# Experts that run by their count: a test around a loop that no expert enters, code moved between instruction pages, and fp32 conversions spread over the experts

## The chip, the cores and the metric

One core of a Trainium2 chip. The time is the device time of one launch in microseconds (us); of several runs the median counts. Five engines work side by side, each with its own list of instructions: PE (TensorE, matmuls; PEld is its weight load), DVE (VectorE), ACT (ScalarE), POOL (GpSimd) and SP (SyncE). They wait for each other through semaphores only. Loads and stores go through DMA queues that SP, ACT and POOL feed. The code of an engine comes through a DMA queue of its own too (q8 and q14 in the profile).

## The reference

Three layers in a row over 2304 tokens of 512 numbers; arithmetic in fp32.

```python
# 1. attention: B, H, S, D = 4, 8, 576, 64; each query sees the 64 keys up to itself
scores = where((rel >= 0) & (rel < 64), q @ k.T / sqrt(D), -1e9)
x = softmax(scores) @ v                    # to [2304, 512]
# 2. experts: 8 of them, FF 1024
do = x @ w_skip > 0                        # other tokens pass unchanged
e_idx = argmax(x @ w_gate); p = softmax(x @ w_gate)
x[do] += p[e_idx] * (relu(x[do] @ w1[e_idx]) @ w2[e_idx])
# 3. a last feed-forward layer, 512 to 2048 to 512, for all tokens
h = x @ w_in
out = where(h >= 1, h, where(h <= -1, 0, (h + 1)**2 / 4)) @ w_out
```

How many tokens an expert has is known only at run time. With these inputs expert 2 has more than 128 and at most 256, expert 4 more than 256 and at most 384, the other six at most 128.

## The kernel before

Attention and the routing of the tokens come first (to 117.6 us), then the experts (to 276.1), a transition (to 287), and the last layer, which takes the rest. At the very start PE runs WARM matmuls of WARM_COLUMNS columns on ones while the first loads come in.

**Experts.** The tokens of an expert are cut into tiles of 128. `tile_of(e, t)` runs a tile t of expert e through `ffn`: the matmuls `ha` and `hb` with w1 (L753), ACT's relu that evacuates them (`h`, L760), their transposes (`hTp`, L766), the matmuls `y` with w2 (L792), and `mx`, which adds the weighted result to the tokens (DVE, L797). `load_x` gathers a tile's tokens by index, `store_x` scatters them back, both on POOL's DMA queue. Tile 0 of each expert always runs. Tile 1 stands in an If on the expert's count (L860), tile 2 in a second (L864), and further tiles in a For_i whose bounds are `3 * P` and the count (L868). In the built program these are branches on each engine: the instructions are all there, and an engine whose expert has no such tile jumps over them, on PE some 390 instructions for L860.

**fp32 by parts.** Every fp32 operand of a matmul is split into a high and a low part that add up to it: ACT writes the high part (L132 and L137), DVE, in some cases POOL, the low one (L133 and L138). `hT` and `mxT` are such splits of a tile's data, `w` those of weights. The splits of weights are ahead of their use by a ring of 14 pairs, and are laid out by the hooks of `ffn`: functions that are called at fixed places of a tile 0 ("start", "a", "b", 0, 1, 2) and put instructions there. `mine` are the pairs of this expert's second half, `nxt` those of the next expert, `splits` the first seven left over.

**Conversions.** The weights of the last layer (w_in, w_out, named `raw` when loaded) come as 64-bit numbers, and eight pieces of them are converted to fp32 during the experts: `convert` is five DVE operations on 128x512 each (L168; before, the first two run through a generator, `convert_by_parts`, L191 and L168). SLOW says how many of the pieces in EARLY are converted by expert e: those from SLOW[e] to SLOW[e+1]. They run in hook "a" and, if left, in hook 2; the two first ones in expert 0 by hook "start" and "b".

**Order of loads.** `to_load` is a list of the pieces in order of need, and `load_raws` starts the next when a buffer is free: on SP's queue, twice on ACT's in the beginning.

**Code.** An engine's instructions stand in the order of the Python code; the loop bodies of later tiles are part of it, at each expert. All of it lies in DRAM and comes to the engine in pieces.

Of the kernel before, what the change touches and what calls it, by code (L numbers as in the profile page):

```python
# [4 lines left out]

# [6 lines left out]
F32 = mybir.dt.float32  # L12
F32R = mybir.dt.float32r
BF16 = mybir.dt.bfloat16
I32 = mybir.dt.int32
I64 = mybir.dt.int64
AF = mybir.ActivationFunctionType
# [31 lines left out]

EARLY = tuple((U_IN + j, c) for j in range(2) for c in range(4))  # L50
EARLIEST = 2
BEFORE = 6

LATE = tuple(
    (u, c) for u in (U_OUT, U_OUT + 1, U_IN + 2, U_OUT + 2, U_IN + 3, U_OUT + 3) for c in range(4)
)
AHEAD_OF_IT = 3

SLOW = (2, 4, 5, 6, 6, 7, 8, 8, 8)
ROUTES = (3, 3, 3, 3, 3, 3)  # L60
WARM = 97
WARM_COLUMNS = 80
WGW = 32
AHEAD = 3
KEEP = (4, 8, 70, 2, 36)
# [5 lines left out]
def moe_chain(  # L71
# [54 lines left out]
    def take_raw(key):  # L126
        r, n = raws.pop(key)
        left[n] = max(left.values(), default=0) + 1
        return r
# [12 lines left out]
    def convert_ops(w, r, mag=None):  # L142

        low, high = r[:, :, 0], r[:, :, 1]
        wf = w.bitcast(F32)
        v = nc.vector
        ops = [
            partial(  # L150
                v.tensor_scalar, w, high, 3, 0x3FFFFFFF, op0=ALU.logical_shift_left, op1=ALU.bitwise_and
            ),
            partial(
                v.scalar_tensor_tensor, w, high, -0x40000000, w, op0=ALU.bitwise_and, op1=ALU.bitwise_or
            ),
            partial(
                v.scalar_tensor_tensor, w, low, 29, w, op0=ALU.logical_shift_right, op1=ALU.bitwise_or
            ),
        ]
        if mag is None:  # L160
            ops.append(partial(v.tensor_single_scalar, high, high, 0x7FFFFFFF, ALU.bitwise_and))
            mag = high.bitcast(F32)
        ops.append(partial(v.scalar_tensor_tensor, wf, mag, LEAST, wf, op0=ALU.is_ge, op1=ALU.mult))
        return ops
# [13 lines left out]
    def do_convert(u, c, into):  # L178
# [1 line left out]
            early[u, c] = into.tile([P, 2, 512], F32, tag="early", name=f"c{u}_{c}")  # L180
        convert(early[u, c // 2 * 2][:, c % 2].bitcast(I32), take_raw((u, c)))
        load_raws()

    def convert_by_parts(todo, into):

        for _, u, c in todo:
            if c % 2 == 0:
                early[u, c] = into.tile([P, 2, 512], F32, tag="early", name=f"c{u}_{c}")
            for op in convert_ops(early[u, c // 2 * 2][:, c % 2].bitcast(I32), raws[u, c][0]):
                yield  # L190
                op()  # L191
            take_raw((u, c))
            if at_once[0]:
                load_raws()

    def work(todo, engines):

        for eng in engines[: len(todo)]:
            what, u, c = todo.pop(0)
            if what == "s":  # L200
                do_split(u, c, eng)
            else:
                do_convert(u, c, early_pool[0])
# [495 lines left out]
    with ExitStack() as ectx:  # L699
# [3 lines left out]
        def bank(i, shape, name):  # L703
            return psp.tile(shape, F32, tag=f"bank{i}", name=name)
# [7 lines left out]
        def load_x(at, name, tag, bufs):  # L712
            x = mp.tile([P, RW], F32, tag=tag, name=f"mx{name}", bufs=bufs)
            nc.gpsimd.memset(tick, 0.0)
            dma = nc.gpsimd.indirect_dma_start(
                out=x, out_offset=None, in_=x1,
                in_offset=bass.IndirectOffsetOnAxis(ap=at, axis=0),
            )
            apart(dma, "gathers", ("scatters",))
            return x  # L720
# [17 lines left out]
            split(xT[:, 0], xT[:, 1], px)  # L738
            return xT

        def ffn(e, x, xT, name, hooks=(), b0=0):

            hooks = dict(hooks)

            def at(k):
                if k in hooks:
                    hooks[k]()

            def mm1(ph, j, lo, hi):
                seq = [(c, a, b) for p in (PASSES[:2], PASSES[2:]) for c in range(KD) for a, b in p]  # L750
                for n in range(lo, hi):
                    c, a, b = seq[n]
                    nc.tensor.matmul(  # L753
                        ph, lhsT=xT[:, a, c, :], rhs=halves[4 * e + j, c][:, b, :],
                        start=(n == 0), stop=(n == len(seq) - 1),
                    )

            def evac(ph, j):
                h = mp.tile([P, 512], F32, tag="h", name=f"h{name}_{j}")
                nc.scalar.activation(h, ph, AF.Relu)  # L760
                return h

            def tr(h, j):
                pt = bank(b0 + j, [P, 4, P], f"hTp{name}_{j}")
                for c in range(4):
                    nc.tensor.transpose(pt[:, c, :], h[:, c * P : (c + 1) * P], ident)  # L766
                hT = mp.tile([P, 2, 4, P], F32R, tag=f"hT{j}", name=f"hT{name}_{j}", bufs=1)
                split(hT[:, 0], hT[:, 1], pt)
                return hT

            at("start")
            pa = bank(b0, [P, 512], f"ha{name}")
            mm1(pa, 0, 0, 12)
            ha = evac(pa, 0)
            pb = bank(b0 + 1, [P, 512], f"hb{name}")
            mm1(pb, 1, 0, 6)
            hTa = tr(ha, 0)
            at("a")
            mm1(pb, 1, 6, 12)
            hb = evac(pb, 1)  # L780
            py = bank(b0 + 2, [P, 512], f"y{name}")
            hT = [hTa, None]

            seq = [(c, a, b) for p in (PASSES[:2], PASSES[2:]) for c in range(4) for a, b in p]
            for j in range(2):
                for n, (c, a, b) in enumerate(seq):
                    if j == 0 and n == 6:
                        hT[1] = tr(hb, 1)
                        at("b")
                    if j == 1 and n % 3 == 0:  # L790
                        at(n // 3)
                    nc.tensor.matmul(  # L792
                        py, lhsT=hT[j][:, a, c, :], rhs=halves[4 * e + 2 + j, c][:, b, :],
                        start=(j == 0 and n == 0), stop=(j == 1 and n == len(seq) - 1),
                    )
            y = x[:, 0:DM]
            nc.vector.scalar_tensor_tensor(y, py, x[:, DM:RW], y, op0=ALU.mult, op1=ALU.add)  # L797
# [14 lines left out]

        rawp.append(ectx.enter_context(tc.tile_pool(name="raw2", bufs=RAWS[2])))
        early_pool.append(ectx.enter_context(tc.tile_pool(name="earlier", bufs=len(EARLY) // 2)))
        parts = convert_by_parts(converts, early_pool[0])
        fetch(0, 0)
        work(splits, [dve] * 3)
        pre(0, 0)
# [8 lines left out]
        for e in range(NE):  # L827

            mine = pairs(8 * e + RING - 8, 8 * e + 8)
            nxt = pairs(8 * e + 8, 8 * e + RING)  # L830
            if e == 0:
                mine, nxt = [], []
            elif e + 1 == NE:
                nxt = [("s", u, c) for u, c in EARLY if c % 2 == 0]
            turn = [("c", u, c) for u, c in EARLY[SLOW[e] : SLOW[e + 1]]]
            last = e + 1 == NE
            def second():

                xeT[e, 1] = mp.tile([P, 2, KD, P], F32R, tag="mxT", name=f"mxT{e}_1")
                with tc.If(counts[e] > P):  # L840
                    prep(xe[e, 1], f"{e}_1", "mxTl", xeT[e, 1])

            hooks = {
                "start": lambda: (
                    work(splits, [dve] * len(splits)),
                    list(islice(parts, BEFORE)) if e == 0 else None,
                    work(mine, [dve, dve]),
                ),
                "a": lambda: (
                    work(turn, [dve]),  # L850
                    work(nxt, [dve, dve] if last else [dve]),
                ),
                "b": lambda: (list(parts) if e == 0 else None, work(nxt, [dve, dve])),
                0: lambda: None if last else (pre(e + 1, 0), fetch(e + 1, 1)),
                1: lambda: (second(), work(nxt, [dve, dve])),
                2: lambda: (work(nxt, [dve]), work(turn, [dve])),
            }
            tile_of(e, 0, hooks)
            store_x(at_of(e, 0), xe[e, 0])
            with tc.If(counts[e] > P):  # L860
                fetch(e, 2)
                tile_of(e, 1)
                store_x(at_of(e, 1), xe[e, 1])
                with tc.If(counts[e] > 2 * P):  # L864
                    pre(e, 2)
                    tile_of(e, 2)
                    store_x(at_of(e, 2), xe[e, 2])
                    with tc.For_i(3 * P, counts[e], P) as r:  # L868
                        at = mp.tile([P, 1], I32, tag="at", name=f"at{e}", bufs=1)
                        nc.vector.tensor_copy(at, idx[:, bass.ds(r // P + e * NT, 1)])  # L870
                        x = load_x(at, f"{e}_l", "mxl", 1)
                        ffn(e, x, prep(x, f"{e}_l", "mxTl"), f"{e}_l", b0=4)
                        store_x(at, x)
            if e + AHEAD < NE:
                fetch(e + AHEAD, 0)

# [280 lines left out]
```

## Time and profile before

| | |
|---|---|
| median of 3 runs | 709.76 us (709.02 to 711.63) |
| the profiled execution: its time | 707.99 us |
| the profiled execution: its span | 706.3 us |
| attention and routing | 117.6 us |
| experts | 158.5 us |
| transition | 10.9 us |
| last layer | 419.3 us |

The span is the time from the first to the last instruction in the profile; the run's own time is 1.7 us longer. Times in the views are us from the span's start. `PEclk` is the granted TensorE clock as a share of full speed. A wait "<- issue" is one in which the profile shows nothing that the engine waited for.

### The profile page before, as it was taken

How to read it: one execution, taken by the hardware profiler on the slowest of the kernel's cores; microseconds unless marked ns; L12 is line 12 of the kernel's file. 1: busy time of each engine (PE TensorE's matmuls, PEld its weight loads, DVE VectorE, ACT ScalarE, POOL GpSimd, SP SyncE). 2: the span in 40 equal slices, each digit the busy share in tenths (PEclk: the TensorE clock that was granted, in tenths of full speed). 3: DMA queues.
4: the chain of work that ended last, by engine and by line, in shares of the span. 5: the costliest groups of instructions: out<-in, count | busy, mean ns of one | idle time of the engine just before them, and what ended most of it. 6: DMA issues, size and time to landing. Idle time of an engine off the chain costs nothing.

```text
span 706.3 us, 12298 instructions
## 1 busy us (share of the span) xinstructions
PE 672.3 (95%) x4622; PEld 573.1 (81%) x4622; DVE 426.4 (60%) x806; ACT 384.5 (54%) x765; POOL 92.6 (13%) x137
## 2 busy tenths in 40 slices
PE   7999977899999799998999999999999999999997
PEld 6777766677787575897989999999999999999995
DVE  4788864997782499787888864444433443333332
ACT  5787642374761485565666655454444454445443
POOL 3256545031230211000000000000000000000000
PEclk9999998999999999999999999999999999999999
DMA  8999944898791393632423202120300030002002
GB/s 210 312 277 290 301 149 112 282 329 329 214 356 59 113 314 122 213 110 76 148 87 94 76 0 61 31 59 31 91 1 0 1 90 0 1 1 45 1 1 45
DMA packets 34502, 88.81 MB, mean 126 GB/s; under 512 B 6958, under 2 KB 8110, under 8 KB 34420
## 3 DMA queue, kind: packets, MB, share of 16 engines
q1 hardware_dynamic: 25344, 71.72, 33.7%
q10 hardware_dynamic: 6756, 9.45, 3.9%
q0 software_dynamic: 2320, 6.58, 2.7%
q8 instruction: 47, 0.77, 0.5%
q14 instruction: 35, 0.29, 0.1%
HBM read 75.65 MB, written 13.12 MB: 126 GB/s over the span
## 4 chain that ended last, share of the span: by engine, by line
PE 55%; DVE 3%; ACT 1%; issue 1%; ACTq 0%; DVEq 0%
PE h L914 27%; PE po L942 26%; PE spare L1030 1%; PE p2x L904 1%; DVE c L935 1%; DVE c L932 1%; ACT q L925 1%; DVE w L138 0%; DVE gs L933 0%; DVE q L924 0%; DVE x2T L133 0%; ACT q L921 0%; DVE q L928 0%; ACT part L951 0%; ACT w L137 0%
## 5 line engine op out<-in xcount | busy, mean ns | idle before, releaser
L914 PE MATMUL h<-x2T,w 128*128 128x384 f32 x1152 | 218.2, 338 | 1.0 <-DVE x2T L133 0.9
L942 PE MATMUL po<-w,gs 128*128 128x512 f32 x864 | 217.3, 396 | 1.6 <-ACT w L137 0.9
L914 PEld LDWEIGHTS h<-x2T,w 128*128 128x128 f32 x1152 | 204.7, 188 | 10.0 <-DVE x2T L133 1.7
L942 PEld LDWEIGHTS po<-w,gs 128*128 128x128 f32 x864 | 159.6, 188 | 32.0 <-ACT w L137 1.2
L921 ACT ACTIVATE q<-h 128x384 f32<-128x384 f32 x96 | 47.0, 489 | 107.8 <-PE h L914 106.5
L924 DVE TENSOR_SCALAR q<-q 128x384 f32<-128x384 f32 x96 | 34.4, 358 | 98.2 <-ACT q L921 98.0
L928 DVE TENSOR_TENSOR q<-hs,q 128x384 f32<-128x384 f32 x96 | 53.7, 559 | 49.8 <-ACT q L925 49.8
L930 ACT ACTIVATE gs<-q 128x384 fp32r<-128x384 f32 x96 | 50.5, 526 | 60.0 <-DVE q L928 60.0
L933 DVE TENSOR_TENSOR gs<-q,gs 128x384 fp32r<-128x384 f32 x96 | 53.6, 559 | 44.4 <-ACT gs L930 44.4
L137 ACT ACTIVATE w<-raw 128x1024 fp32r<-128x1024 f32 x64 | 65.1, 1057 | 26.2 <-issue 12.1
L792 PE MATMUL y<-w,hT 128*128 128x512 f32 x264 | 69.7, 403 | 1.8 <-DVE hT L133 0.7
L138 DVE TENSOR_TENSOR w<-raw,w 128x1024 fp32r<-128x1024 f32 x54 | 63.6, 1220 | 12.0 <-ACT w L137 10.0
L925 ACT ACTIVATE q<-q 128x384 f32<-128x384 f32 x96 | 50.5, 526 | 22.6 <-DVE q L924 19.1
L792 PEld LDWEIGHTS y<-w,hT 128*128 128x128 f32 x264 | 47.4, 189 | 14.5 <-issue 3.3
L360 ACT ACTIVATE pr<-s,nb 128x128 f32<-128x128 f32 x144 | 39.0, 383 | 17.0 <-DVE nb L356 17.0
L923 ACT ACTIVATE hs<-h 128x384 f32<-128x384 f32 x96 | 46.8, 487 | 0.0
L753 PE MATMUL ha<-w,mxT 128*128 128x512 f32 x132 | 35.4, 417 | 9.8 <-issue 4.9
L753 PEld LDWEIGHTS ha<-w,mxT 128*128 128x128 f32 x132 | 25.1, 197 | 19.3 <-issue 10.6
L753 PE MATMUL hb<-w,mxT 128*128 128x512 f32 x132 | 35.2, 402 | 0.0
L356 DVE TENSOR_REDUCE nb<-s 128x4 f32<-128x512 f32 x36 | 23.2, 686 | 14.8 <-PE s L349 12.5
L724 POOL DMA_INDIRECT x<-mx,idx x11 | 16.5, 1501 | 116.6 <-POOLq L860 65.1
L138 POOL TENSOR_TENSOR w<-raw,w 128x1024 fp32r<-128x1024 f32 x10 | 23.6, 2362 | 35.7 <-ACT w L137 24.7
(172 smaller groups left out, 690.9 us busy)
## 6 DMA issues: line engine op xcount, KB each, us to landing
raw<-in_wu SPq DMA_DIRECT2D x62, 512.0 KB, 6.2
raw<-in_wd SPq DMA_DIRECT2D x28, 512.0 KB, 4.0
x<-x ACTq DMA_DIRECT2D x21, 256.0 KB, 6.1
vt<-in_vs SPq DMA_DIRECT2D x36, 130.0 KB, 6.3
x<-x SPq DMA_DIRECT2D x18, 256.0 KB, 3.2
out<-out SPq DMA_DIRECT2D x36, 128.0 KB, 2.4
q<-in_qs SPq DMA_DIRECT2D x8, 512.0 KB, 5.7
kt<-in_ks SPq DMA_DIRECT2D x8, 512.0 KB, 6.9
```

The costliest lines, as they stand in the source:

```text
L137: nc.scalar.activation(t[:, 0], src, AF.Copy)
L138: eng.tensor_tensor(t[:, 1], src, t[:, 0].bitcast(F32), ALU.subtract)
L753: nc.tensor.matmul(ph, lhsT=xT[:, a, c, :], rhs=halves[4 * e + j, c][:, b, :], start=(n == 0), stop=(n == len(seq) - 1),)
L792: nc.tensor.matmul(py, lhsT=hT[j][:, a, c, :], rhs=halves[4 * e + 2 + j, c][:, b, :], start=(j == 0 and n == 0), stop=(j == 1 and n == len ...
L914: nc.tensor.matmul(ph, lhsT=halves[U_IN + m // 4, c][:, b, (m % 4) * P : (m % 4 + 1) * P], rhs=xT[:, a, c, :], start=(n == 0), stop=(n == ...
L921: nc.scalar.activation(q, ph, AF.Relu, bias=0.5, scale=0.5)
L923: nc.scalar.activation(h, ph, AF.Copy)
L925: nc.scalar.activation(q, q, AF.Square)
L928: nc.vector.tensor_tensor(q, h, q, ALU.max)
L930: nc.scalar.activation(gs[:, 0], q, AF.Copy)
L933: dve.tensor_tensor(gs[:, 1], q, gs[:, 0].bitcast(F32), ALU.subtract)
L942: nc.tensor.matmul(po[i], lhsT=gs[:, a, i * P : (i + 1) * P], rhs=w[:, b, :], start=(m == m0 and (a, b) == PASSES[0]), stop=(m == m1 - 1 a ...
```

## The change

Seven edits, of which most touch the experts:

1. The loop of tiles 3 and on stands in an If of its own, `counts[e] > 3 * P`, and counts from 0.
2. Its body uses whole fp32 operands (`prep_whole`, `mm1_whole`) instead of split ones, so it has fewer matmuls. No expert has such a tile.
3. WARM is 115 and WARM_COLUMNS 64, instead of 97 and 80.
4. SLOW spreads the conversions: by expert 0 to 7 they are 0, 1, 1, 1, 1, 1, 1, 1, 0 pieces by SLOW instead of 2, 1, 1, 0, 1, 1, 0, 0 (the first two pieces come on top, both in expert 0).
5. The first two conversions are whole ones in hook "b" and hook 1, no generator of parts any more.
6. In expert 0 the leftover weight splits stand in hook "a" instead of "start".
7. The order of loads follows SLOW.

```diff
-BEFORE = 6
...
-SLOW = (2, 4, 5, 6, 6, 7, 8, 8, 8)
+SLOW = (2, 2, 3, 4, 5, 6, 7, 8, 8)
 ROUTES = (3, 3, 3, 3, 3, 3)
-WARM = 97
-WARM_COLUMNS = 80
+WARM = 115
+WARM_COLUMNS = 64
...
+        def prep_whole(x, name):
+            px = bank(7, [P, KD, P], f"mpx{name}")
+            for c in range(KD):
+                nc.tensor.transpose(px[:, c, :], x[:, c * P : (c + 1) * P], ident)
+            xT = mp.tile([P, 2, KD, P], F32, tag="mxTl", name=f"mxT{name}", bufs=1)
+            nc.scalar.activation(xT[:, 0], px, AF.Copy)
+            return xT
...
+            def mm1_whole(ph, j):
+                w = xT[:, 1].rearrange("p c n -> p (c n)")
+                for c in range(KD):
+                    half = halves[4 * e + j, c].bitcast(F32)
+                    nc.vector.tensor_tensor(w, half[:, 0, :], half[:, 1, :], ALU.add)
+                    nc.tensor.matmul(ph, lhsT=xT[:, 0, c, :], rhs=w, start=(c == 0), stop=(c == KD - 1))
...
-        parts = convert_by_parts(converts, early_pool[0])
...
             hooks = {
-                "start": lambda: (
+                "start": lambda: work(mine, [dve, dve]),
+                "a": lambda: (
                     work(splits, [dve] * len(splits)),
-                    list(islice(parts, BEFORE)) if e == 0 else None,
-                    work(mine, [dve, dve]),
-                ),
-                "a": lambda: (
                     work(turn, [dve]),
                     work(nxt, [dve, dve] if last else [dve]),
                 ),
-                "b": lambda: (list(parts) if e == 0 else None, work(nxt, [dve, dve])),
+                "b": lambda: (work(converts, [dve]), work(nxt, [dve, dve])),
                 0: lambda: None if last else (pre(e + 1, 0), fetch(e + 1, 1)),
-                1: lambda: (second(), work(nxt, [dve, dve])),
+                1: lambda: (second(), work(converts, [dve]), work(nxt, [dve, dve])),
                 2: lambda: (work(nxt, [dve]), work(turn, [dve])),
             }
...
-                    with tc.For_i(3 * P, counts[e], P) as r:
...
+                    with tc.If(counts[e] > 3 * P):
+                        with tc.For_i(0, (counts[e] - (2 * P + 1)) // P, 1) as i:
...
+                            ffn(e, x, prep_whole(x, f"{e}_l"), f"{e}_l", b0=4, whole=True)
```

The order on DVE in expert 0 before: from the program's list of DVE's instructions, from the start of the tile to its last conversion but one. `raw` is a loaded piece, `c` the converted one, `hT_0_0` and `hT_0_1` the two halves of expert 0's tile 0, `mxT` the next tiles' data.

```order
L138 TENSOR_TENSOR w_2_2468<-raw_2_1864,w_2_2468 128x1024
L191 TENSOR_SCALAR c_0_2473<-raw_0_1983 128x512
L191 SCALAR_TENSOR_TENSOR c_0_2473<-raw_0_1983,c_0_2473 128x512 x2
L133 TENSOR_TENSOR hT_0_0_2508<-hTp_0_0_2503,hT_0_0_2508 128x512
L168 TENSOR_SCALAR c_2_2511<-raw_2_2372 128x512
L133 TENSOR_TENSOR hT_0_1_2539<-hTp_0_1_2534,hT_0_1_2539 128x512
L191 TENSOR_SCALAR c_0_2473<-raw_1_2370 128x512
L133 TENSOR_TENSOR mxT_0_2560<-mpx_0_2555,mxT_0_2560 128x512
L168 TENSOR_SCALAR c_2_2511<-raw_3_2374 128x512
L797 SCALAR_TENSOR_TENSOR mx_0_2350<-y_0_2527,mx_0_2350 128x512
```

Each `TENSOR_SCALAR c` row begins one conversion; rows of its other operations are left out. The same stretch in the changed program (its L131 is L133 here, L136 is L138, L166 is L168, L803 is L797):

```order
L131 TENSOR_TENSOR hT_0_0_2513<-hTp_0_0_2508,hT_0_0_2513 128x512
L136 TENSOR_TENSOR w_2_2516<-raw_2_1882,w_2_2516 128x1024
L131 TENSOR_TENSOR hT_0_1_2541<-hTp_0_1_2536,hT_0_1_2541 128x512
L166 TENSOR_SCALAR c_0_2544<-raw_0_2001 128x512
L131 TENSOR_TENSOR mxT_0_2563<-mpx_0_2558,mxT_0_2563 128x512
L166 TENSOR_SCALAR c_0_2544<-raw_1_2388 128x512
L803 SCALAR_TENSOR_TENSOR mx_0_2368<-y_0_2529,mx_0_2368 128x512
```

Of four conversions two are left in expert 0, both behind `hT_0_1`; the weight split moved behind `hT_0_0`.

DVE in expert 6 in the changed program, the first half of tile 0: before, the list is the same without the four rows of L166.

```order
L131 TENSOR_TENSOR hT_0_0_5040<-hTp_0_0_5035,hT_0_0_5040 128x512
L166 TENSOR_SCALAR c_2_4621<-raw_3_4632 128x512
L166 SCALAR_TENSOR_TENSOR c_2_4621<-raw_3_4632,c_2_4621 128x512 x2
L166 TENSOR_SCALAR raw_3_4632<-raw_3_4632 128x512
L166 SCALAR_TENSOR_TENSOR c_2_4621<-raw_3_4632,c_2_4621 128x512
L136 TENSOR_TENSOR w_0_5050<-raw_0_4660,w_0_5050 128x1024
L131 TENSOR_TENSOR hT_0_1_5073<-hTp_0_1_5068,hT_0_1_5073 128x512
```

One conversion came in between the halves of `hT`. Expert 3 gained one at the same place.

PE at the end of expert 4's tile 2 in the program before: the entry of the loop, its first and its last matmuls, and the first of expert 5.

```order
L792 MATMUL y_2_4369<-w_2_4103,hT_2_1_4381 128x512 x2
L868 COMPARE_AND_BRANCH
L868 UNCONDITIONAL_BRANCH x2
L1153 BRANCH_PREFETCH_HINT
L733 MATMUL mpx_l<-ident,mx_l 128x128 x4
```

The changed program at the same place:

```order
L870 COMPARE_AND_BRANCH
L871 REGISTER_ALU x2
L871 COMPARE_AND_BRANCH
L871 UNCONDITIONAL_BRANCH x2
L1156 BRANCH_PREFETCH_HINT
```

The branch of the new If (L870) stands ahead of everything that belongs to the loop (L871).

## Rows read from the trace of the kernel before

**Rows 1.** The page's first line.

```profile
span 706.3 us, 12298 instructions
```

**Rows 2.** Stretch, us, busy PE, PEld, DVE, ACT, POOL, clock, DMA share, GB/s.

```profile
117.60:276.10 158.50, 144.27 (x660) 111.44 (x661) 114.30 (x140) 85.73 (x112) 34.50 (x51) 0.99 0.71 243
...
287.00:706.30 419.30, 411.63 (x2090) 371.34 (x2088) 216.26 (x412) 220.50 (x448) 0.00 (x0) 1.00 0.17 50
```

**Rows 3.** PE's longest wait in 117.6 to 276.2: total us, times, longest.

```profile
PE ha L753 <- issue: 4.9, 1, 4.9
```

**Rows 4.** Timeline of PE: start, us, instructions, idle before and releaser.

```profile
135.37 3.04 PE L753 MATMUL ha<-w,mxT 128*128 128x512 f32 x12 [1.81 <-PEq L860]
...
139.63 0.60 PE L766 MATMUL hTp<-ident,h 128*128 128x128 f32 x4
...
165.68 1.21 PE L753 MATMUL ha<-w,mxT 128*128 128x512 f32 x4 [0.40 <-DVE mxT L133]
...
176.50 3.05 PE L753 MATMUL ha<-w,mxT 128*128 128x512 f32 x12 [0.43 <-PEq L864]
...
204.91 1.19 PE L753 MATMUL ha<-w,mxT 128*128 128x512 f32 x4 [0.17 <-DVE mxT L133]
...
233.97 4.62 PE L753 MATMUL ha<-w,mxT 128*128 128x512 f32 x12 [4.85 <-issue]
...
276.13 7.93 PE L1030 MATMUL spare<-ones 128*128 128x512 bf16 x36 [0.99 <-DVEq L860]
```

**Rows 5.** A stretch behind PE's longest gap, columns as in group 2.

```profile
234.20:237.70 3.50, 3.50 (x9) 2.70 (x9) 2.36 (x2) 1.37 (x2) 2.73 (x3) 0.51 0.16 42
```

**Rows 6.** Lines L860, L868: instructions, ns min/median/max, first and last start.

```profile
L860 PEldq COMPARE_BRANCH  x8: 70/412/2972, 132.2 to 272.9; - x8
L868 PEldq EVENT_SEMAPHORE  x13: 51/51/1615, 229.2 to 233.6; - x13
```

**Rows 7.** The page's queue of PE's code: packets, MB, share.

```profile
q8 instruction: 47, 0.77, 0.5%
```

**Rows 8.** Three stretches of the experts, columns as in group 2.

```profile
128.00:165.70 37.70, 34.10 (x159) 25.35 (x157) 36.40 (x52) 22.83 (x29) 9.20 (x12) 1.00 0.89 317
188.50:204.90 16.40, 16.09 (x77) 12.60 (x75) 15.87 (x21) 13.13 (x17) 4.59 (x6) 1.00 0.97 325
241.10:275.20 34.10, 32.95 (x152) 25.07 (x150) 32.25 (x36) 27.12 (x34) 5.27 (x6) 1.00 0.69 234
```

**Rows 9.** Timeline of DVE: start, us, instructions, idle before and releaser.

```profile
128.63 0.42 DVE L168 TENSOR_SCALAR c<-raw 128x512 int32<-128x512 int32 x1
...
131.49 0.69 DVE L133 TENSOR_TENSOR hT<-hTp,hT 128x512 fp32r<-128x512 f32 x1
...
141.87 0.68 DVE L133 TENSOR_TENSOR hT<-hTp,hT 128x512 fp32r<-128x512 f32 x1
...
183.05 1.22 DVE L138 TENSOR_TENSOR w<-raw,w 128x1024 fp32r<-128x1024 f32 x1 [0.26 <-ACT w L137]
185.33 0.69 DVE L133 TENSOR_TENSOR hT<-hTp,hT 128x512 fp32r<-128x512 f32 x1 [1.05 <-ACT hT L132]
186.28 2.36 DVE L138 TENSOR_TENSOR w<-raw,w 128x1024 fp32r<-128x1024 f32 x2 [0.26 <-ACT w L137]
...
241.12 0.69 DVE L133 TENSOR_TENSOR hT<-hTp,hT 128x512 fp32r<-128x512 f32 x1 [4.10 <-ACT hT L132]
...
272.26 2.36 DVE L138 TENSOR_TENSOR w<-c,w 128x1024 fp32r<-128x1024 f32 x2 [0.26 <-ACT w L137]
...
275.18 0.75 DVE L797 SCALAR_TENSOR_TENSOR mx<-y,mx 128x512 f32<-128x512 f32 x1 [0.55 <-PE y L792]
```

**Rows 10.** Timeline of ACT in expert 0, its half of `hT`.

```profile
128.44 0.60 ACT L132 ACTIVATE hT<-hTp 128x512 fp32r<-128x512 f32 x1 [1.22 <-PE hTp L766]
```

**Rows 11.** PE at the start, the warm-up and its first wait for a load.

```profile
1.12 5.68 PE L590 MATMUL warm<-ones 128*128 128x80 bf16 x97 [1.12 <-DVE ones L212]
...
14.57 1.10 PE L349 MATMUL s<-kt,q 64*64 64x128 f32 x32 [0.34 <-DMA kt<-in_ks]
```

More of the change, by code (lines that the diff above doesn't have):

```diff
@@ L3 @@
 from functools import partial
-from itertools import islice
 import concourse.bass as bass
@@ L182, in do_convert @@
         load_raws()
[L184 to L194, printed above, removed]
     def work(todo, engines):
@@ L739, in prep, with ffn @@
             return xT
-        def ffn(e, x, xT, name, hooks=(), b0=0):
+        def prep_whole(x, name):
[5 more added lines that the diff above has]
+            return xT
+        def ffn(e, x, xT, name, hooks=(), b0=0, whole=False):
             hooks = dict(hooks)
@@ L747, in at @@
                     hooks[k]()
+            def mm1_whole(ph, j):
[4 more added lines that the diff above has]
+                    nc.tensor.matmul(ph, lhsT=xT[:, 0, c, :], rhs=w, start=(c == 0), stop=(c == KD - 1))
             def mm1(ph, j, lo, hi):
+                if whole:
+                    if lo == 0:
+                        mm1_whole(ph, j)
+                    return
                 seq = [(c, a, b) for p in (PASSES[:2], PASSES[2:]) for c in range(KD) for a, b in p]
@@ L867, in moe_chain @@
                     store_x(at_of(e, 2), xe[e, 2])
-                    with tc.For_i(3 * P, counts[e], P) as r:
[L869 to L873, printed above, removed]
+                    with tc.If(counts[e] > 3 * P):
+                        with tc.For_i(0, (counts[e] - (2 * P + 1)) // P, 1) as i:
+                            at = mp.tile([P, 1], I32, tag="at", name=f"at{e}", bufs=1)
+                            nc.vector.tensor_copy(at, idx[:, bass.ds(i + (e * NT + 3), 1)])
+                            x = load_x(at, f"{e}_l", "mxl", 1)
+                            ffn(e, x, prep_whole(x, f"{e}_l"), f"{e}_l", b0=4, whole=True)
+                            store_x(at, x)
             if e + AHEAD < NE:
```

## The prediction

> **What bounds the kernel now.** The page gives a span of 706.3 us [rows 1], one core; the profiled run took 707.99 us, the median of three 709.76. The question is where PE is idle and which of that this change can reach. The span is cut into stages first. The last stage, 419 us, has PE busy 411.63 of 419.30 [rows 2], and the diff leaves it alone: it counts as unchanged and only shifts. The first 117.6 us change only in the warm-up. Everything else lies in the experts, 117.6 to 276.1 us, where PE is idle 14.2 of 158.5 us. The list of PE's waits for that stage begins with 4.9 us in one piece before `ha`, with no releaser shown ("issue") [rows 3].
>
> The timeline of PE [rows 4] places the long ones. The 1.81 us come at 135.37, between expert 0 and 1; the 4.85 us at 233.97, between expert 4 and 5. [...] So the gap costs twice: 4.85 idle, then 4.62 − 3.04 = 1.58 of slow matmuls.
>
> Why does PE wait there? The instructions of L868 [rows 6] show PE going through 13 semaphores between 229 and 234 us, the longest 1.6 us; the other engines have such lists too. Only an expert with more than 256 rows reaches the loop; this happens once, and its body runs no time at all. It is a meeting of all engines before a loop of zero trips.
>
> And the 1.81 us? PE's branch at L860 takes 0.07 us at the least, 0.41 in the median of eight, and once 2.97 [rows 6]. The instruction queue q8 moved 0.77 MB in 47 packets, 16 KB each [rows 7]; at 64 bytes an instruction that is 256 of PE's. Counted in the built program, expert 0's branch stands at PE's instruction 3831, in piece 14, and goes to 4221, in piece 16 counted from 0: it leaps over one piece. Every other skip lands in the same piece or the next.
>
> Last, VectorE. Three windows show it without slack up to a point where PE waits for it: 36.40 of 37.70 us until PE waits 0.40 for `mxT` at 165.68, 15.87 of 16.40 until PE waits 0.17 at 204.91, and 32.25 of 34.10 before `mx` of expert 7 at 275.18 [rows 4, 8, 9].
>
> **The change part by part, against the span of 706.3.**
>
> *The test before the loop.* Expert 4 now skips the loop's meeting. What stays is one more skip; the one of L864 left PE idle 0.43 at 176.50 [rows 4]. I take 0.50: 4.85 to 0.50 is −4.35. With no such gap the twelve matmuls of `ha` should run at 3.04: −1.58. Bounds: the gap shrinks only by the longest single wait, 1.6, and the clock still falls (−1.6); or all goes, 4.85 + 1.58 = −6.4. `ha` of expert 5 needs `mxT` and two splits which DVE had finished before the gap (DVE idles 4.10 behind it [rows 9], so no backlog is hidden there): I take −5.93.
>
> *The page leap.* WARM is 115 instead of 97 matmuls, with a weight load each: 36 PE instructions more ahead of all branches. Expert 0's branch then stands at 3867 (piece 15), its target at 4249 (piece 16), and I find no leap over a piece in the new program; on the other engines neither. The stall falls from 1.81 to what other skips cost PE; with target data ready I take 0.15, so −1.66. Bounds: 0 if what delayed that branch is no matter of pieces, −1.81 at the other end.
>
> [...]
>
> *Conversions.* One is five DVE operations, 0.42, 2 × 0.69, 0.42 and 0.69 with overlap: from the first one's start at 128.63 to the next instruction at 131.49 that is 2.86 us [rows 9]; I use 2.85. By expert 0 to 6 the old order has 4, 1, 1, 0, 1, 1, 0 of them, the new 2, 1, 1, 1, 1, 1, 1. They only cost where DVE has no slack, so I take the three stretches.
>
> Experts 0 to 2: expert 0 loses two conversions, 5.7 us of DVE's work, but DVE then waits for the first `hT` of expert 1. PE's `ha` starts earlier: at 135.37 it waits only on the branch; the tile's last products end at 135.37 − 1.81 = 133.56 [rows 4], so it begins at about 133.6. Its transposes stood 4.26 us behind it (139.63) and take 0.60 [rows 4], ACT's half another 0.60 as at 128.44 [rows 10]: `hT` of expert 1 can come at 139.1 by PE and ACT. DVE's own chain begins with `hT` 0_1, which stood at 131.49 behind conversions and is now released by ACT's half at 128.44 + 0.60 [rows 9, 10]: 129.0, then this `hT` 0.6, two conversions 5.7, `mxT` and `mx` 0.6 + 0.7, two splits 2.35, gaps 0.4: about 139.3. Before, `hT` of expert 1 stood at 141.87 [rows 9]: −2.5. From there DVE's queue runs on without gaps to the `mxT` that PE waits for at 165.68, so PE arrives there 2.5 earlier, and the page leap's 1.66 is inside this number, not beside it. If the leap's stall stays, `ha` begins at 135.37 as before, `hT` comes at 140.9 and this is −1.0. On ACT the raw loads that it issues change (one more of w_in), and a split of a weight leaves from ahead of the evacuation of `h`: work of one kind comes, of the other goes, and DVE's queue, not ACT's, sets `hT` of expert 1: nothing.
>
> Expert 3 gains a conversion behind `hT` 3_0. DVE's idle time that can swallow it, 0.26 + 1.05 + 0.26, is 1.57 [rows 9]; 2.85 − 1.57 = +1.29 goes to PE at 204.91. Bounds: nothing if ACT is late by that much anyway, +2.85 if none of the idle is usable.
>
> Expert 6 gains one too. From `hT` of expert 5 at 241.12 to `mx` at 275.18 DVE's waits that I can see are 0.55 and 0.26, 0.81 [rows 9]; 2.85 − 0.81 = +2.04. After `mx` come the scatter and the reload of x1, on which the last stage starts; the 36 warm matmuls, 7.93 us [rows 4], only fill the time. Bounds: 0 and +2.85.
>
> *Warm-up.* 115 × 64 columns against 97 × 80 are 0.95 of the columns; the 97 matmuls took 5.68 us, 59 ns each [rows 11]. By columns 5.68 becomes 5.4, by count at unchanged spacing 6.7: −0.3 to +1.05. Behind it PE waits 0.34 for `kt` at 14.57 [rows 11], so a small shift is absorbed: 0.
>
> *The loop's body* with whole fp32 weights never runs; it shortens the code that is skipped by 8 instructions: nothing.
>
> Sum: −5.93 − 2.5 + 1.29 + 2.04 + 0 = −5.1. Span 701.2, the run's own time 702.9; on the median of the runs shown, which lies 1.77 above that run, 709.76 − 5.1 = 704.7.
>
> **The rivals.**
>
> *The two added conversions cost nothing.* If ACT rather than DVE is late in experts 3 and 6, the +1.29 and +2.04 fall away: −8.4, 701.3 us. For it: 1.05 us of DVE's idle in expert 3 are waits on ACT. Against: DVE's windows are 95 to 97% full.
>
> *The clock falls later.* In expert 7 PE would wait for `mx` up to 0.99 + 2.04 = 3.03 us instead of 0.99 before its warm matmuls. If PE's clock falls there as it did behind 4.85 us of idle, its matmuls lose about what `ha` lost: +1.4, 706.1 us. Against: 1.81 us at 135.37 were followed by 3.04 for twelve, at full speed.
>
> *The leap's stall stays* (what delayed that one branch was something else): −2.5 becomes −1.0, 706.2 us. For it: one case alone shows the stall, and its cause is inferred. Against: the median of the eight branches is 0.41 us [rows 6]. [...]
>
> *The meeting only moves.* The new If has an end of its own; if engines meet there as at L868, gap and slow clock stay: +5.93 − 5.1 = +0.8, 710.6 us. Against: the Ifs at L860 and L864 are of the same kind, and L864's cost PE 0.43 [rows 4].
>
> *Slower.* With the code shifted, the skips of the other experts could be the ones that leap a piece: if the stall of expert 0 stays and six more have one, that is −3.6 + 6 × 1.66 = +6.4, 716.2 us. It is slower from three more on, and by more than half a percent from five. For it: branch distances are alike in all experts, so a cut of the pieces that hits one can hit several. Against: counted as above, none leaps; the pieces would have to be cut elsewhere than I count.
>
> **How the numbers follow.** The sum as worked out: 0.50, its own range 703 to 706. Added conversions free: 0.14. The clock falls: 0.18. The stall stays: 0.08. The meeting moves: 0.06. Slower: 0.04. The median moves by half a percent at 3.55 us, about what a measurement of this kernel can tell from no change; faster means below 706.2. Forecast and first rival are faster (0.64), the cases at 706.1 and 706.2 lie at the edge and about half of each counts as faster (0.14); the other half and the moved meeting are the same (0.18). The range of 701.0 to 707.3 takes in the free conversions below, and above the cases at 706 with 1.05 us for what the warm-up can add; it leaves out the moved meeting and the slower case and some of both ends, under 0.2.
>
> **What would show it.** PE's idle between expert 4 and 5 under 1 us and twelve `ha` matmuls in about 3.0 there; no instruction at the loop's line with long semaphore waits. The branch between expert 0 and 1 under 0.5 us. `hT` of expert 1 on DVE near 139.3 and PE's `ha` near 163.2 where it continued at 165.68. The distance between PE's tiles in expert 3 and 4 longer by 1.3, the wait of `spare` longer by up to 2. The last stage 419.3 long. Wrong would be: an `ha` of expert 5 that still waits, or waits for DVE instead; a slow clock in the last stage; warm matmuls that end after 7.5 us with nothing to absorb them.

## The result, and the profile after

The changed kernel takes 719.62 us (median of 4, 716.07 to 720.73) against 709.39 for the one before: a ratio of 1.0132 with a 95% interval of 1.0088 to 1.0176. It is slower, by about 10 us, where 5.1 us faster was forecast. The profiled execution took 719.37 us, its span is 717.6.

Stretches of the kernel after (columns as in group 2 of the rows above): the experts, the transition, the last layer, each from its first instruction on PE.

```profile
121.45:285.97 164.52, 146.15 (x656) 113.61 (x657) 115.25 (x140) 84.91 (x111) 28.23 (x48) 0.97 0.69 231
285.97:296.81 10.84, 10.84 (x58) 5.75 (x58) 9.87 (x16) 3.53 (x5) 1.18 (x1) 1.00 0.62 199
296.81:717.50 420.69, 413.22 (x2090) 372.34 (x2088) 216.16 (x412) 220.55 (x448) 0.00 (x0) 0.99 0.18 49
```

From the first `ha` to the warm matmuls at their end the experts took 157.1 us before (119.03 to 276.13) and take 164.5 now. The first `ha` comes 2.4 us later and the last layer is 1.4 longer. In the 14 profiles of this study the first `ha` comes anywhere from 116.9 to 123.8, in four kernels with one and the same warm-up (experiments 9 to 12) from 116.9 to 120.7, and the last layer, whose code was not changed, takes 419.3 to 421.2. One profile of each kernel therefore does not show these two differences to be effects of the change. The 7.4 us in the experts are what the experiments below explain.

PE's waits there, in total, times, longest:

```profile
PE hTp L772 <- ACT h L766: 14.0, 6, 3.2
PE ha L759 <- PEq L870: 0.4, 1, 0.4
```

What was forecast to go has gone. The 4.9 us before `ha` of expert 5 [rows 3] are 0.4, the wait behind L860 (now L862) between expert 0 and 1 is off the list. In its place stands a wait that was 1.4 us before, for ScalarE's relu `h`, with 14.0. The timeline of PE shows it in experts 1, 2, 4, 6 and 7 (another 0.69 in expert 0 is like the 1.03 there before):

```profile
135.59 3.03 PE L759 MATMUL ha<-w,mxT 128*128 128x512 f32 x12
...
141.70 0.66 PE L772 MATMUL hTp<-ident,h 128*128 128x128 f32 x4 [1.68 <-ACT h L766]
...
158.28 0.66 PE L772 MATMUL hTp<-ident,h 128*128 128x128 f32 x4 [3.15 <-ACT h L766]
158.69 2.13 PE L759 MATMUL hb<-w,mxT 128*128 128x512 f32 x6
160.62 2.66 PE L798 MATMUL y<-w,hT 128*128 128x512 f32 x6
...
202.04 0.66 PE L772 MATMUL hTp<-ident,h 128*128 128x128 f32 x4 [3.17 <-ACT h L766]
...
237.06 3.05 PE L759 MATMUL ha<-w,mxT 128*128 128x512 f32 x12 [0.42 <-PEq L870]
...
257.86 0.66 PE L772 MATMUL hTp<-ident,h 128*128 128x128 f32 x4 [3.16 <-ACT h L766]
...
274.99 0.66 PE L772 MATMUL hTp<-ident,h 128*128 128x128 f32 x4 [2.12 <-ACT h L766]
```

The matmuls of `ha` of expert 1 start in time: 14.1 us behind the first `ha`, where it was 16.3 before and the forecast had 14.6. But their result is not taken away. Why relu is late is seen on ACT:

```profile
139.16 2.00 ACT L135 ACTIVATE w<-raw 128x1024 fp32r<-128x1024 f32 x2 [6.23 <-DVEq L862]
141.07 0.58 ACT L766 ACTIVATE h<-ha 128x512 f32<-128x512 f32 x1
...
155.74 2.00 ACT L135 ACTIVATE w<-raw 128x1024 fp32r<-128x1024 f32 x2 [4.03 <-DVEq L862]
157.65 0.58 ACT L766 ACTIVATE h<-ha 128x512 f32<-128x512 f32 x1
```

Relu stands behind two weight splits of the hook "start", and the first of them waits for "DVEq L862": for a semaphore from VectorE's sequencer, behind the branch of the expert before. The semaphore instructions at this line start at 135.5 on PE. On VectorE the branch stands at 137.8, but the semaphores behind it only at 139.0, when `mx`, which adds the result to the tokens, has ended (138.27 + 0.74):

```profile
138.27 0.74 DVE L803 SCALAR_TENSOR_TENSOR mx<-y,mx 128x512 f32<-128x512 f32 x1
...
L862 PEldq COMPARE_BRANCH  x8: 73/412/451, 133.2 to 282.7; - x8
L862 DVEq COMPARE_BRANCH  x8: 49/56/63, 137.8 to 285.0; - x8
L862 PEldq EVENT_SEMAPHORE  x6: 51/51/51, 135.5 to 285.0; - x6
L862 DVEq EVENT_SEMAPHORE  x6: 21/21/21, 139.0 to 285.8; - x6
```

The program's list says what ACT's first split of expert 1 waits for, before and after:

```
L137 ACTIVATE w_0_2868<-raw_0_2376 128x1024 [waits DMAHW0_49,PE_49]
L135 ACTIVATE w_0_2883<-raw_0_2390 128x1024 [waits DMAHW6_49,DVE_49,PE_49]
```

VectorE is new there. The split writes a slot of the ring that held the first w1 pair of expert 0. In the loop's new body VectorE adds the two halves of exactly those pairs (`mm1_whole`). No expert enters the body, but in this program the slot is only free once every engine that may read it has passed the place where it would, and for VectorE that is behind `mx`.

Behind the waits in experts 2, 6 and 7 the next matmuls are slow as well: in expert 2 `hb` takes 2.13 and `y` 2.66 us, where six take 1.64 and 1.55 in expert 1; in experts 6 and 7 six `hb` take 2.64 and 2.70. The granted clock is 0.70 in 160 to 165, between the 0.51 of [rows 5] and 1.00:

```profile
160.00:165.00 5.00, 5.00 (x19) 3.88 (x19) 4.80 (x8) 2.36 (x4) 0.24 (x2) 0.70 0.94 314
```

### The profile page after: what moved, and what is told of

The parts are those of the page before. It is cut to its first block, busy times and chain, and to the rows that moved or that the text cites. A ratio compares the mean times of both kernels' runs of the same rounds, so it can differ in the third digit from the quotient of the medians.

```text
span 717.6 us, 12265 instructions
## 1 busy us (share of the span) xinstructions
PE 678.0 (94%) x4640; PEld 577.8 (81%) x4640; DVE 426.7 (59%) x806; ACT 384.5 (54%) x765; POOL 87.8 (12%) x137
## 4 chain that ended last, share of the span: by engine, by line
PE 50%; DVE 6%; ACT 2%; issue 1%; DMA 0%; ACTq 0%; DVEq 0%
PE po L945 24%; PE h L917 24%; DVE c L938 2%; PE spare L1033 1%; ACT q L928 1%; DVE gs L936 1%; PE p2x L907 1%; DVE c L935 1%; DVE w L136 1%; DVE q L927 1%; DVE q L931 1%; DVE x2T L131 0%; DMA x<-x 0%; ACT q L924 0%; ACT gs L933 0%
## 5 line engine op out<-in xcount | busy, mean ns | idle before, releaser
L798 PE MATMUL y<-w,hT 128*128 128x512 f32 x264 | 71.3, 411 | 0.9
L136 DVE TENSOR_TENSOR w<-raw,w 128x1024 fp32r<-128x1024 f32 x54 | 63.6, 1220 | 10.3 <-ACT w L135 9.4
L798 PEld LDWEIGHTS y<-w,hT 128*128 128x128 f32 x264 | 49.7, 196 | 13.2 <-issue 3.3
L926 ACT ACTIVATE hs<-h 128x384 f32<-128x384 f32 x96 | 46.7, 487 | 0.0
L759 PE MATMUL hb<-w,mxT 128*128 128x512 f32 x132 | 37.7, 424 | 0.0
L759 PE MATMUL ha<-w,mxT 128*128 128x512 f32 x132 | 33.2, 400 | 3.2 <-ACT mxT L130 1.5
L131 DVE TENSOR_TENSOR hT<-hTp,hT 128x512 fp32r<-128x512 f32 x22 | 15.2, 690 | 27.9 <-ACT hT L130 22.6
L759 PEld LDWEIGHTS hb<-w,mxT 128*128 128x128 f32 x132 | 25.3, 198 | 5.3
```

The lines of the kernel that those rows point to most:

```text
L136: eng.tensor_tensor(t[:, 1], src, t[:, 0].bitcast(F32), ALU.subtract)
L759: nc.tensor.matmul(ph, lhsT=xT[:, a, c, :], rhs=halves[4 * e + j, c][:, b, :], start=(n == 0), stop=(n == len(seq) - 1),)
L798: nc.tensor.matmul(py, lhsT=hT[j][:, a, c, :], rhs=halves[4 * e + 2 + j, c][:, b, :], start=(j == 0 and n == 0), stop=(j == 1 and n == len ...
L926: nc.scalar.activation(h, ph, AF.Copy)
```

## The experiments

Ratios are against the kernel before, measured beside each experiment on the same chip, each with its 95% interval. Experiments 1 to 4, 5 to 8 and 9 to 12 ran on three chips, so between these groups ratios are compared and not times.

**1. Another engine reads in the body.** One line of the body that never runs:

```diff
-                    nc.vector.tensor_tensor(w, half[:, 0, :], half[:, 1, :], ALU.add)
+                    nc.scalar.activation(w, half[:, 0, :], AF.Copy)
```

> The changed kernel, with one line of the loop body that never runs altered: the operand that VectorE added from the two halves of a weight is a copy of the high half by ScalarE (the body would leave the low part out; no expert enters it). Theory A (release): the body makes VectorE a reader of the ring of weight pairs, so ScalarE's first split of the next expert waits until VectorE has passed the expert's branch, and relu behind it waits too. By A PE's 14.0 us of waits for h fall to the 1.4 of before and the clock dips in experts 3, 6 and 7 go: 704 to 709 us. Theory B (conversions): the conversions spread over the experts make VectorE and with it ScalarE late: the waits stay and the time is 716 to 720.

705.41 us, ratio 0.9909 (0.9878 to 0.994). The experts take 151.18 us instead of 164.52, PE's waits for `h` are 1.0, and the clock is 1.00 throughout:

```profile
PE hTp L772 <- ACT h L766: 1.0, 2, 0.7
...
122.71:273.89 151.18, 142.54 (x656) 109.94 (x657) 114.01 (x140) 85.16 (x111) 32.51 (x48) 1.00 0.73 252
```

So one line that is never executed costs 13.3 us of the experts: 9.7 of PE's idle time (18.4 against 8.6) and 3.6 of longer matmuls (146.15 against 142.54 busy). Without it the change is about as much faster as was forecast. Theory B falls: the spread conversions are all in this kernel.

**2. The body alone.** The kernel before with `prep_whole`, `mm1_whole` and the new warm-up, nothing else.

> The kernel before, with the loop body on whole weights and the new warm-up (115 x 64) alone; conversions and loop as before. Theory A: ScalarE's first split of an expert waits for VectorE's branch here too, PE waits for h some 8 to 14 us more than the 1.4 of before, 715 to 721 us. Theory B: nothing of this, 707 to 710 us.

724.01 us, ratio 1.0166 (1.0128 to 1.0204), which is above the 715 to 721 expected. The experts take 170.3 us in the profile, 157.7 in experiment 4, which differs from this by the body and the exact warm-up; the test that gives some 6 us back in the changed kernel is missing. PE's waits for `h` are as expected, and ACT's first split of expert 1 waits for VectorE. Besides, four branches, in experts 3, 5, 6 and 7, take 1.1 to 3.3 us:

```profile
PE hTp L786 <- ACT h L780: 14.3, 7, 3.8
...
144.02 2.00 ACT L137 ACTIVATE w<-raw 128x1024 fp32r<-128x1024 f32 x2 [8.48 <-DVEq L880]
...
L880 PEldq COMPARE_BRANCH  x8: 70/768/3323, 136.7 to 290.5; - x8
```

**3. The test around the loop alone,** with the new warm-up.

> The kernel before with the test around the loop and the new warm-up alone; conversions and split weights as before. By count three branches of PE now leap over a 16 KB piece of its code, those of experts 5, 6 and 7, and that of expert 0 no longer does. If the test removes the meeting: PE idle between expert 4 and 5 under 1 us, the twelve matmuls behind it in about 3.0, -5.9; with three leaps of 1.7 us that is 706 to 710 us, without leaps' cost 703 to 705. If the meeting moves: the gap stays at 4 us or more and the time at 709 to 712.

711.91 us, ratio 0.9998 (0.9971 to 1.0024). The meeting is gone (0.43 us before expert 5, 3.04 for twelve matmuls), and its gain is spent on stalls at branches:

```profile
233.12 3.04 PE L753 MATMUL ha<-w,mxT 128*128 128x512 f32 x12 [0.43 <-PEq L868]
...
249.73 4.59 PE L753 MATMUL ha<-w,mxT 128*128 128x512 f32 x12 [3.51 <-PEq L860]
265.85 3.02 PE L753 MATMUL ha<-w,mxT 128*128 128x512 f32 x12 [1.51 <-PEq L860]
...
L860 PEldq COMPARE_BRANCH  x8: 73/338/5209, 135.7 to 276.8; - x8
```

The three branches that leap over a piece of code by count, in experts 5, 6 and 7, took 5.21, 3.61 and 3.28 us; no other took over 0.4. PE stands idle 3.51 and 1.51 us behind the first two, and twelve matmuls behind the first take 4.59 us instead of 3.04: 6.6 us together. The total is 2 us above the 706 to 710 expected: the leaps cost more than the 1.7 us each put in.

**4. Only the placement of code.**

```diff
-WARM = 97
-WARM_COLUMNS = 80
+WARM = 102
+WARM_COLUMNS = 76
```

> The kernel before with 102 warm-up matmuls of 76 columns instead of 97 of 80, the same columns in all: by count no branch of PE leaps over a piece of code any more. If the leap made the stall, PE's idle before the first ha of expert 1 falls from 1.81 to under 0.5 us, and the time to 707 to 709.5 (VectorE's queue, without gaps there, gives back most of it). If the stall has another cause it stays at 1.8 us, and so does the time.

710.28 us, ratio 0.9984 (0.9954 to 1.0014). No branch takes over 0.45 us now, where one took 2.97 [rows 6], and the 1.81 us of idle are gone:

```profile
L860 PEldq COMPARE_BRANCH  x8: 70/326/451, 134.2 to 274.8; - x8
```

The time does not move measurably. From the first `ha` to the one that waits for `mxT` (165.68 before, 167.67 here) it is 46.7 us before and 47.3 here, so the idle time that went gave PE nothing there. This fits the expectation that VectorE's queue, with the old conversions, sets the pace up to that point and gives most of it back.

**5. The old conversions, otherwise as experiment 1.**

> As e1_act_reader (test around the loop, ScalarE instead of VectorE in the body that never runs, the new warm-up), but the conversions and expert 0's splits as in the kernel before. By the sum on record the new conversions are worth -2.5 in experts 0 to 2, +1.3 in 3 and 4, +2.0 in 5 to 7, so +0.8 in all: this kernel 0.8 us faster than e1_act_reader, near 704.5 on the runs of before of 711. If the added conversions are hidden, it is 2.5 us slower, 708.

703.32 us, ratio 0.9917 (0.989 to 0.9944): by the total no difference to 0.9909 can be told. The stretches tell more. PE in this kernel, and then in the one of experiment 1:

```profile
119.56 3.06 PE L773 MATMUL ha<-w,mxT 128*128 128x512 f32 x12 [0.81 <-ACT mxT L132]
...
165.89 1.20 PE L773 MATMUL ha<-w,mxT 128*128 128x512 f32 x4 [0.40 <-DVE mxT L133]
...
205.10 1.19 PE L773 MATMUL ha<-w,mxT 128*128 128x512 f32 x4 [0.20 <-DVE mxT L133]
...
269.85 7.93 PE L1051 MATMUL spare<-ones 128*128 128x512 bf16 x36 [0.99 <-DVEq L880]
```

```profile
122.71 3.05 PE L759 MATMUL ha<-w,mxT 128*128 128x512 f32 x12 [0.84 <-ACT mxT L130]
...
166.18 1.21 PE L759 MATMUL ha<-w,mxT 128*128 128x512 f32 x4 [0.41 <-DVE mxT L131]
...
206.42 1.19 PE L759 MATMUL ha<-w,mxT 128*128 128x512 f32 x4 [0.40 <-DVE mxT L131]
...
273.89 7.93 PE L1033 MATMUL spare<-ones 128*128 128x512 bf16 x36 [1.11 <-DVEq L862]
```

From mark to mark 46.33, 39.21 and 64.75 us with the old conversions, 43.47, 40.24 and 67.47 with the new: −2.9, +1.0 and +2.7. Of the last, 2.0 lie in experts 6 and 7 (13.20 and 14.18 us long with the old conversions, 14.06 and 15.36 with the new), the rest in the later tiles of expert 4.

**6. The old warm-up, otherwise as experiment 1.**

> As e1_act_reader, but with the warm-up of before (97 x 80). Expert 0's branch leaps over a piece of code again. If a leap is a stall: the branch takes 2.5 to 5 us there, PE idles 1.5 us or more before expert 1, time +1.0 to +2 against e1_act_reader. If the new warm-up costs more at the start than the leap (PE waited 1.2 to 2.1 us for nothing that is shown near 30 us in two profiles with it): 0 to -2.

705.08 us, ratio 0.993 (0.9903 to 0.9957), not to be told from experiment 1 by the total. The branch of expert 0 takes 2.35 us, a little under the 2.5 to 5 expected, but PE idles only 0.26 us behind it, where 1.5 or more was expected. And four more branches take 1.4 to 3.7, which do not leap over a piece by count:

```profile
L862 PEldq COMPARE_BRANCH  x8: 73/1652/3662, 131.4 to 271.4; - x8
...
133.97 3.03 PE L759 MATMUL ha<-w,mxT 128*128 128x512 f32 x12 [0.26 <-PEq L862]
...
148.96 4.34 PE L759 MATMUL ha<-w,mxT 128*128 128x512 f32 x12 [1.96 <-PEq L862]
```

A leap over a piece stands at every stall of the kernel before and of experiment 3, but not at these four, nor at the four of experiment 2. With the five stalls the experts take 154.8 us, 3.6 more than in experiment 1.

**7. The splits behind relu.** The changed kernel, with the work of "start" moved:

```diff
-                "start": lambda: work(mine, [dve, dve]),
                 "a": lambda: (
+                    work(mine, [dve, dve]),
```

> The changed kernel, VectorE still the reader in the body, but the two splits of the hook start moved into hook a, behind relu of ha and the halves of hT. Theory A in full says that the harm is what stands behind the waiting split on ScalarE, relu above all: PE's waits for h fall from 14.0 to under 3 us and the time comes to 0.988 to 0.995 of before. If the late split itself is the harm (the weights of the second half come too late for y): waits for w or for h stay, 1.005 to 1.02.

717.44 us, ratio 1.0112 (1.0082 to 1.0141). What theory A was to give here, waits under 3 us and 0.988 to 0.995, did not come; the time lies in the range of the other case. The trace shows why: the splits no longer wait, but three of them, 2.94 us, now stand together ahead of relu of `hb`, and PE waits there, in experts that had no such wait too. The run thus puts one delay in the place of another and does not decide between the two cases:

```profile
140.10 2.94 ACT L135 ACTIVATE w<-raw 128x1024 fp32r<-128x1024 f32 x3
142.95 0.59 ACT L766 ACTIVATE h<-hb 128x512 f32<-128x512 f32 x1
...
PE hTp L772 <- ACT h L766: 11.5, 7, 2.6
```

The place at the start, while ACT has nothing else to do, was the right one; it only must not wait.

**8. GpSimd reads in the body** (`nc.gpsimd` for `nc.vector` in the line of experiment 1).

> The changed kernel with GpSimd instead of VectorE adding the halves in the body that never runs. GpSimd passes an expert's branch behind VectorE (139.33 and 139.05 in the changed kernel), since it waits for mx before the scatter. Theory A: ScalarE's first split waits for GpSimd's branch, the waits for h are 14 us or more, 1.012 to 1.022 of before. If VectorE as such were the trouble (its load or its queue): 0.99 to 1.0.

720.92 us, ratio 1.0177 (1.0144 to 1.021). VectorE has no part in it, and the wait has moved to the new reader, a little longer:

```profile
136.62 2.00 ACT L135 ACTIVATE w<-raw 128x1024 fp32r<-128x1024 f32 x2 [6.68 <-POOLq L862]
```

**9 and 10. Which half is read.** The body with whole weights for `hb` only, and for `ha` only; the core is one condition, with j the half of w1 (j == 1 in experiment 9, j == 0 in 10). A second tile for the whole operand takes the place of an `hT`.

```diff
-                if whole:
+                if xW is not None and j == 1:
```

> The changed kernel, but in the body that never runs only hb (the second half of w1) uses whole weights added by VectorE, ha uses split ones as before; the warm-up is 103 x 72 so that by count no branch of PE leaps over a piece of code. The ring slots that ScalarE fills first in the next expert are those of ha, so VectorE no longer reads them. Theory A: waits for h back to some 1 us, experts 150 to 153 us, 0.988 to 0.994 of before. If any reading of the ring by VectorE in the body does the harm: 1.005 to 1.015.

> The counterpart: only ha uses whole weights added by VectorE, hb split ones, same warm-up. Theory A: VectorE reads just the slots that are filled first, so the whole harm is there: waits for h 12 to 15 us, 1.008 to 1.018. If the harm goes with the number of reads: half of it, about 1.0.

For `hb`: 702.6 us, ratio 0.9922 (0.9893 to 0.9951), experts 150.47. For `ha`: 715.4 us, ratio 1.0094 (1.0066 to 1.0122), experts 163.8. The two programs have the same number of instructions and VectorE additions; only the slots read differ. PE's waits for `h` are 0.7 us in 9 and 13.5 in 10. In the program's list VectorE's semaphore, DVE_49, stands at ACT's first split of expert 1 in 10 and not in 9; the split in 9 and in 10:

```profile
131.16 2.01 ACT L135 ACTIVATE w<-raw 128x1024 fp32r<-128x1024 f32 x2 [2.65 <-PEq L864]
```

```profile
134.20 2.00 ACT L135 ACTIVATE w<-raw 128x1024 fp32r<-128x1024 f32 x2 [6.24 <-DVEq L864]
```

Kernel 9 leaves nothing out of the body, and beats both kernels.

**11. The conversions where VectorE is idle,** otherwise as 9: `SLOW = (2, 2, 3, 5, 5, 7, 8, 8, 8)`.

> As g1_second_half_whole, with the conversions by expert 0 to 6 at 2, 1, 2, 0, 2, 1, 0: expert 0 as in the change, none added in experts 3 and 6, the two left put where later tiles leave VectorE idle (experts 2 and 4). By the stretches of f1_old_conversions and e1_act_reader the change gains 2.9 us in experts 0 to 2 and gives back 1.0 in 3 and 4 and 2.7 in 5 to 7: this one should keep the first and not pay the others, 3 to 4 us under g1_second_half_whole. If the conversions in experts 2 and 4 are on the path too: no gain.

705.56 us, ratio 0.9938 (0.9914 to 0.9961), against 0.9922 for 9: no gain, where 3 to 4 us were expected. Tile 0 of experts 4, 6 and 7 is 0.8 to 1.2 us shorter than in 9, as expected. But the second tile of expert 2 is 1.1 us longer (11.88 against 10.81) and the two later tiles of expert 4 4.5 longer, with a gather that lands later:

```profile
211.74 3.96 PE L800 MATMUL y<-w,hT 128*128 128x512 f32 x16 [0.82 <-DVE hT L131]
217.58 0.63 PE L719 MATMUL mpx<-ident,mx 128*128 128x128 f32 x4 [1.88 <-DMA mx<-x,idx]
```

**12. The old conversions, otherwise as 9.**

> As g1_second_half_whole with the conversions and expert 0's splits of the kernel before. By the same stretches 0.8 us faster than g1_second_half_whole; 3 us slower if the added conversions are hidden.

702.22 us, ratio 0.9908 (0.9876 to 0.994), against 0.9922 for 9: too small to be told by the total. Nor do the profiles bear out the sum of 0.8: the experts take 151.0 us here and 150.5 in 9. The new conversions make −3.7, +1.0 and +2.1 in the three stretches of experiment 5.

## Why the prediction was wrong

The step that failed is the one on the loop's body: that it "never runs; it shortens the code that is skipped by 8 instructions: nothing". It looked at what the body issues and not at what it reads. In this program a reader makes its engine one that the next refill of the slot waits for, run or not: ACT stood idle before its first split of expert 1 for 6.23 us until VectorE released it in the changed kernel, 6.68 until GpSimd did in experiment 8, and 2.65 until PE did in experiment 9. Experiments 1, 8 and 10 against 9 show it by changing only the reader or only the slot, and experiment 2 shows it with no other edit than the warm-up beside it. By experiment 1 the term is +13.3 us in the experts, against a forecast of 0; −5.1 + 13.3 is +8.2, and the experts lost 7.4.

It could have been priced from the rows of before. ACT's two splits at expert 1, and VectorE's `mx` ahead of its branch, in the kernel before:

```profile
135.35 2.01 ACT L137 ACTIVATE w<-raw 128x1024 fp32r<-128x1024 f32 x2 [4.31 <-PEq L860]
138.50 0.60 ACT L760 ACTIVATE h<-ha 128x512 f32<-128x512 f32 x1 [1.15 <-PE ha L753]
...
138.63 0.75 DVE L797 SCALAR_TENSOR_TENSOR mx<-y,mx 128x512 f32<-128x512 f32 x1
```

The splits began when PE was past its branch; `mx` ended at 139.4. Two splits of 1.0 us from 139.4 put relu at 141.4, where PE had produced `ha` by 138.5: 3 us a time (1.7 to 3.2 came), for each expert whose predecessor has one tile only. In experts 3 and 5, behind experts 2 and 4 with later tiles, no such wait came. The estimate leaves out the slow matmuls behind some of the waits.

The other terms, from experiments with the wait taken away:

- *The test before the loop:* right. −5.93 forecast; from the first `ha` of expert 4's last tile to that of expert 6 it is 31.85 us before (17.07 + 14.78), and 25.87 in experiment 5 (12.64 + 13.23): −6.0. Behind it the twelve `ha` take 3.05 us, against 4.62 [rows 4]; in the changed kernel the clock is 1.00 from 235 to 245.
- *The page leap:* the stall went, as forecast, and alone it is worth nothing measurable (experiment 4). Its price is no constant: other leaps took 2.35 to 5.21 us per branch, and PE idled from 0.26 (experiment 6) to 3.51 us behind them (experiment 3), against 2.97 and 1.81 before. The size of a piece is seen in the trace of before: from 390.0 to 690.8 us q8 moved 12 packets of 16 KB while PE went through 3065 matmuls and weight loads, 255 a packet. The count of pieces agrees with experiments 3 and 4, where the stalls came and went with the leaps (a leap of 398 instructions took 5.21 us); it does not account for the stalls without a leap in experiments 2 and 6. By what a leap stalls PE no run shows.
- *Conversions* (by SLOW the new order is 0, 1, 1, 1, 1, 1, 1, 0, one entry for each of the eight experts): −2.9, +1.0 and +2.7 measured in experiment 5, −2.5, +1.29 and +2.04 forecast. Each stretch has the sign and about the size of its term. The sum is not confirmed: it is +0.8 in this pair of profiles, as forecast, and −0.5 in the pair of experiments 9 and 12. The first stretch gains although the leap is absent from both kernels compared; that it comes from VectorE's 5.7 us less work is argued, since edits 4 to 7 were exchanged together. The price of expert 6's conversion came in the tiles of experts 6 and 7 and not in the wait of `spare`, which is 1.11 us in experiment 1.
- *Warm-up:* 0 forecast; 5.73 against 5.68 us [rows 11]. Whether it delays the first `ha` is open: that comes at 118.7 to 123.8 in the seven profiles with 115 x 64 and at 116.9 to 120.7 in the seven others.

The rivals: that the clock falls later was right in kind, but it fell behind waits for `h` (0.70 in 160 to 165), not behind the one before the warm matmuls, which stayed 0.99. The rival "slower" had the right sign by the wrong mechanism: no branch of the changed kernel took over 0.45 us. Experiments 2 and 6, though, show stalls at several branches, as that rival had them, without the leap that it put them down to.

Left open is what stalls branches that do not leap over a piece (experiments 2 and 6); no run was made for it. The totals of one kernel vary from run to run by some 5 us or more (experiment 1: 701.76 to 709.24), for which no cause was sought.

## What to carry to other kernels

Code in an untaken branch is not free (13.3 us of the experts by experiment 1): here a buffer that it reads was released only when the reading engine had passed it, so before adding a reader, look for who writes that slot next, which engine reads late, and what stands behind the waiting instruction. If such a path must read a slot that is refilled early, let it be read by the engine that refills it or by one that passes early, or choose a slot that is refilled later. And a loop of zero trips still made the engines meet here, with PE idle for 4.85 us [rows 4]: a test around it was worth 6 us at that place, and nothing in total where the shifted code stalled at other branches (experiment 3).

## What was not expected of the hardware

A branch of PE over some 390 instructions took 0.3 to 0.45 us in most places and 0.9 to 5.2 us in others. Two programs that differ only in the warm-up, by 36 instructions of PE, had none and five such stalls (experiments 1 and 6). But where the code stood is not all: in experiments 9 to 12 the branch of expert 0 stands at the same PE instruction by count, 3843, and took 1.13, 0.95, 0.91 and 0.45 us.

And the clock fell after waits of 3.15 and 3.16 us in experts 2 and 6 of the changed kernel, and of 2.12 in expert 7 (0.70 in 160 to 165, 0.76 in 255 to 262, 0.74 in 276 to 282), but not after one of 3.17 us in expert 4: it was 1.00 in 200 to 210, and six `hb` took 1.63 us. In experiment 6 matmuls were slow behind shorter waits, of 1.96 and 1.15 us: the twelve `ha` took 4.34 and 4.58 us, where they took 3.03 behind 0.26.
